# A fused attention and mixture-of-experts kernel: the second layer of its middle part in Strassen form

## The chip, the core and the metric

The kernel runs on one core of a Trainium2 chip. The metric is device time in microseconds (us) of one launch, from the median of several runs. TensorE (PE) multiplies matrices, VectorE (DVE), ScalarE (ACT) and GpSimd (POOL) do elementwise work, SyncE (SP) issues most of the DMA transfers.

## What is computed

Causal attention over 4 batches, 8 heads, 576 positions and head size 64, with a local mask (the last 32 positions) on heads 0 to 3 and a strided one (every 32nd position) on heads 4 to 7. Its output, 2304 tokens of 512 channels, goes through four experts:

```python
p = domain_probs / (domain_probs.sum(-1, keepdims=True) + 1e-09)
out = np.zeros((N, D), dtype=np.float32)
for e in range(E):
    h = np.maximum(x @ w1[e], 0.0)
    out += p[:, e:e + 1] * (h @ w2[e])
```

with N = 2304, D = 512, E = 4 and a hidden size of 1024. All is float32.

## The kernel before, in words

**Precision.** Each float32 operand of a matmul is split into a high part (rounded by ACT to the fp32r type) and a low part (the difference, by DVE or POOL). A product takes three passes: high x high, high x low, low x high. `split` (line 816) makes a pair of instructions: the ACT copy and the difference.

**Units and parts.** An expert's hidden size is halved, so there are 8 units of (512 x 512) weights for each layer. The tokens are in three parts of 384, 896 and 1024 (`TA`, `TBS`, lines 361 and 362).

- First stage: attention for all tokens, mixed with both layers for the first 384 tokens (`plan_first`, line 965), in plain form. The attention output of the other tokens stays in SBUF (`xr`, lines 399 and 403).
- Middle part, 896 tokens (`plan_unit`, line 1293; loop at 1407): the first layer in Strassen form. The weight matrix is cut into quarters a11, a12, a22 and the combinations s1 to s4, the tokens into b11, b21, b22 and t1 to t4 (`plan_x`, line 1040); seven products with 2 halves and 6 matmuls of 448 columns each, instead of eight. The second layer is plain (`plan_mm2`, line 947): 7 tiles of 128 tokens, 12 matmuls of 512 columns for each. `accumulate` (line 932) adds the product times the token's probability into the output tile `acc` straight from PSUM.
- Last part, 1024 tokens (`plan_second`, line 1246): both layers in Strassen form with 512 columns. Here the tokens of the second layer lie along the columns, so the result is transposed (`out_t`) and the probability of a token is a row (`late["p"]`, filled by `plan_p`, line 1236). The two units of one expert are added in `acc`, multiplied by the row, and the sums over experts kept in DRAM (`po`): stored by SP for the first expert, added by an accumulating DMA on POOL's queue for the second, read back and added for the third (lines 1220 to 1230). For the fourth the weights are put on the hidden values instead.

**Weights of the last part.** While the middle part works on a unit, the seven split quarters of its first layer (`plan_keep1`, line 873) and of its second (`plan_keep2`, line 880; three plain ones out of `w2t`, four combinations by way of `wv`) are stored to DRAM (`d1`, `d2`). The last part loads them into the tiles of `wt` and into a ring of four tiles (`plan_ring`, line 1176).

**What sets the order.** Nothing is scheduled on the chip. The class `Plan` (line 44) takes every operation with an engine, a duration, tokens that it reads and writes and a priority (the time at which it is due), and `walk` (line 121) plays a list schedule once, when the program is built: at each step the engine that can start first takes the ready operation with the lowest priority value. The matmuls of the experts keep their written order. An operation of kind "VP" goes to DVE or POOL, one of kind "AD" to ACT or DVE, whichever would end first in that play. DMA transfers have a model of the queue (`transfer`, line 223). The order found this way is fixed on each engine; semaphores do the rest. The last part runs the tasks of `TURN` (line 1090) for each unit: seven products of the first layer ("h"), two of them of the unit after ("next"), then seven of the second ("o").

Of the kernel before, what the change touches and what calls it, by code (L numbers as in the profile page):

```python
# [43 lines left out]
class Plan:  # L44
# [8 lines left out]
    DEEP = 1.26  # L53
    ROW = 1.0
# [6 lines left out]
    def __init__(self, banks, mix):  # L61
        self.ops = []
        self.writer = {}
        self.readers = {}
        self.banks = banks
        self.mix = mix
        self.swing = self.SWING

    def add(self, eng, dur, fn, reads=(), writes=(), prio=0.0, bank=None, moe=False, cols=0, xfer=None, two=False, lead=None, lag=0.0):
# [15 lines left out]
        o.idx = len(self.ops)  # L85
# [35 lines left out]
    def walk(self):  # L121
# [206 lines left out]
def attn_moe_kernel(  # L328
# [59 lines left out]
    d1 = {(u, n): dram.tile([P, 2, 2, 256], F32, name=f"d1{u}{n}") for u in range(2 * E) if u != 2 * E - 2 for n in QUART}  # L388
    d2 = {(u, n): dram.tile([P, 2, 2, 256], F32, name=f"d2{u}{n}") for u in range(2 * E) for n in QUART}
    po = [dram.tile([P, 512], F32, name=f"po{i}") for i in range(TBS[1] // P)]  # L390
    dp = dram.tile([TBS[1] // P * E, P], F32, name="dp")
    prT = const.tile([TBS[1] // P * E, P], F32, name="prT")

    mid_pool = tc.tile_pool(name="mid", bufs=1)
# [3 lines left out]
    raws = {1: mid.tile([P, NKD, FH], F32, name="raw1"), 2: mid.tile([P, NKF, DM], F32, name="raw2")}  # L398
# [417 lines left out]
    def split(src, tok, hi, lo, name, z):  # L816

        need = [tok, "late1"] if name in ("s1", "s2", "s4") or name[:2] == "wv" else [tok]
# [33 lines left out]
    def plan_w1(z, step, plain):  # L852

        def t(i):
            return lambda: tmp["s", i]

        if plain:
            plan_quarter(A11, "raw10", "a11", z)
        total(t(0), A21, A22, ["raw10", "raw11"], "ws0", z + step)
        plan_quarter(t(0), "ws0", "s1", z + step)  # L860
        combine(t(1), t(0), A11, ["raw10", "ws0"], "ws1", z + 2 * step)
        plan_quarter(t(1), "ws1", "s2", z + 2 * step)
        if plain:
            plan_quarter(A12, "raw11", "a12", z + 3 * step)
        combine(t(2), A11, A21, ["raw10"], "ws2", z + 4 * step)
        plan_quarter(t(2), "ws2", "s3", z + 4 * step)
        if plain:
            plan_quarter(A22, "raw11", "a22", z + 5 * step)
        combine(t(0), A12, t(1), ["raw11", "ws1"], "ws0", z + 6 * step)
        plan_quarter(t(0), "ws0", "s4", z + 6 * step)  # L870


    def plan_keep1(u, z):
        for n, nm in enumerate(QUART):
            add("SP", 0.4, lambda nm=nm: nc.sync.dma_start(out=d1[u, nm], in_=wt[nm].bitcast(F32)), [nm + "h", nm + "l"], [f"d1{u}{nm}"],
                z + n, xfer=((1.45, 128),))
# [3 lines left out]
    def plan_keep2(u, z, step):  # L880


        for n, (nm, i, j) in enumerate((("a11", 0, 0), ("a12", 0, 1), ("a22", 1, 1))):
# [3 lines left out]
                [f"w2{2 * j + a}{h}" for a in range(2) for h in "hl"], [f"d2{u}{nm}"], z + 2 + n, xfer=((1.6, 512),))  # L887

        def t(i):
            return lambda: tmp["s", i]  # L890

        def keep(n, nm):
            v = n % 2
            split(t((0, 1, 2, 0)[n]), f"ws{(0, 1, 2, 0)[n]}", lambda: late["wv"][v][:, :, 0], lambda: late["wv"][v][:, :, 1], f"wv{v}", z + n * step)
            add("SP", 0.4, lambda: nc.sync.dma_start(out=d2[u, nm], in_=late["wv"][v].bitcast(F32)), [f"wv{v}h", f"wv{v}l"], [f"d2{u}{nm}"],
                z + n * step + 2, xfer=((1.45, 128),))
# [178 lines left out]
    def pm_of(part):  # L1075
        return 6 * (TBS[part - 1] // 2 + 34) / 2400
# [446 lines left out]
```

## Time and profile before

| | us |
|---|---|
| median of 3 runs (lowest, highest) | 792.45 (792.16, 792.56) |
| the profiled execution | 791.97 |
| its span, first to last instruction | 790.2 |
| first stage, 0 to | 193.6 |
| middle part, 193.6 to | 481.2 |
| last part, 481.2 to | 786 |

The profile is of one execution. Busy time is the time in which an engine works on an instruction. A row of grouped instructions gives source line, engine, operation, "output<-inputs" by the program's names, partitions x elements, count, busy time and mean duration of one in ns. Matmuls are pipelined, so one matmul's duration (0.36 or 0.39 us) overlaps with its neighbours'; what one costs is read from the chain, where consecutive ones are merged.

### The profile page before, as it was taken

To read this page: it belongs to the slowest core of one execution; us is meant where nothing else is said; L and a number is where in the kernel's file an instruction comes from. 1 tells how busy PE (TensorE), PEld (TensorE's weight loads), DVE (VectorE), ACT (ScalarE), POOL (GpSimd) and SP (SyncE) were. 2 spreads that over 40 slices of the span, in tenths; PEclk is the share of its full clock that TensorE was granted. 3 is DMA by queue.
4 is the path that set the end of the run, shared out by engine and by line. 5 is a ranking of instruction groups with operands and counts; after the bars stand their busy time and mean duration, and the time that the engine had idled before them with its cause. 6 is when DMAs were issued, how large, how long until landed. Compare 5 with 4: busy or idle time off the path is not lost.

```text
span 790.2 us, 13778 instructions
## 1 busy us (share of the span) xinstructions
PE 780.6 (99%) x5377; PEld 663.9 (84%) x5377; DVE 585.3 (74%) x807; ACT 361.8 (46%) x662; POOL 340.5 (43%) x261
## 2 busy tenths in 40 slices
PE   8999999999999999999999999999999999999997
PEld 5788888899888889898988888888888888888886
DVE  7888867796888586867768592838774867498885
ACT  4645454653534445263535453735273436442330
POOL 6334223682755162534425170307030753086672
PEclk9999999999999999999999999999999999999999
DMA  9777553157779677775952416737683698559525
GB/s 333 282 269 259 204 176 120 60 201 261 292 276 349 204 293 249 281 265 215 318 219 102 160 40 209 294 116 260 202 327 144 232 172 334 198 189 239 200 81 186
DMA packets 73137, 174.09 MB, mean 220 GB/s; under 512 B 5584, under 2 KB 23664, under 8 KB 73072
## 3 DMA queue, kind: packets, MB, share of 16 engines
q1 hardware_dynamic: 70624, 168.91, 59.5%
q0 software_dynamic: 2304, 4.20, 3.3%
q8 instruction: 42, 0.69, 0.3%
q14 instruction: 23, 0.19, 0.1%
q10 hardware_dynamic: 144, 0.11, 0.0%
HBM read 109.22 MB, written 63.98 MB: 219 GB/s over the span
## 4 chain that ended last, share of the span: by engine, by line
PE 97%; DVE 1%; ACT 0%; issue 0%; POOL 0%; DVEq 0%; ACTq 0%
PE mo L1083 23%; PE mo L930 18%; PE ps L1083 18%; PE sc L1083 15%; PE mo L914 9%; PE ps L930 5%; PE sc L930 5%; PE ps L706 2%; PE ps L674 1%; PE sc L562 1%; PE sc L551 1%; PE mo L1429 0%; PE ps L641 0%; DVE wv L820 0%; DVE mx L579 0%
## 5 line engine op out<-in xcount | busy, mean ns | idle before, releaser
L930 PE MATMUL mo<-w2t,h 128*128 128x512 f32 x336 | 80.8, 389 | 0.0
L930 PEld LDWEIGHTS mo<-w2t,h 128*128 128x128 f32 x336 | 63.1, 188 | 13.0
L930 PE MATMUL mo<-w2t,hs 128*128 128x512 f32 x288 | 70.9, 397 | 0.0
L1152 POOL TENSOR_TENSOR Tt1l<-q,Tt1h 128x512 fp32r<-128x512 f32 x8 | 10.3, 1289 | 134.1 <-ACT Tt1h L1151 134.1
L921 DVE SCALAR_TENSOR_TENSOR h<-c,h 128x448 fp32r<-128x448 f32 x48 | 61.6, 1309 | 2.4 <-ACT h L918 1.0
L930 PEld LDWEIGHTS mo<-w2t,hs 128*128 128x128 f32 x288 | 52.8, 188 | 11.3
L820 POOL TENSOR_TENSOR w2t<-raw,w2t 128x512 fp32r<-128x512 f32 x21 | 31.4, 1505 | 61.2 <-ACT w2t L819 51.1
L1115 DVE TENSOR_TENSOR q<-ps,v 128x512 f32<-128x512 f32 x36 | 24.9, 692 | 39.9 <-PE ps L1083 34.8
L819 ACT ACTIVATE w2t<-raw 128x512 fp32r<-128x512 f32 x60 | 37.4, 631 | 32.7 <-PE mo L930 18.8
L820 POOL TENSOR_TENSOR a<-raw,a 128x512 fp32r<-128x512 f32 x17 | 27.7, 1630 | 57.1 <-DVE c L1318 55.3
L939 DVE SCALAR_TENSOR_TENSOR acc<-mo,pr,acc 128x512 f32<-128x512 f32 x45 | 33.5, 745 | 24.1 <-PE mo L930 23.7
L1117 ACT ACTIVATE q<-q 128x512 f32<-128x512 f32 x36 | 22.8, 632 | 54.3 <-DVE q L1115 53.5
L1156 POOL TENSOR_TENSOR q<-q,q 128x512 f32<-128x512 f32 x26 | 38.2, 1470 | 21.4 <-DVE q L1125 13.6
L914 PE MATMUL mo<-xh,a 128*128 128x384 f32 x192 | 45.6, 340 | 0.0
L819 ACT ACTIVATE wv<-tmp 128x512 fp32r<-128x512 f32 x32 | 20.1, 631 | 53.2 <-POOL tmp L827 8.0
L1156 DVE TENSOR_TENSOR q<-q,q 128x512 f32<-128x512 f32 x38 | 41.3, 1099 | 1.8 <-POOL Tb21l L1152 1.1
L930 PE MATMUL ps<-w2t,h 128*128 128x512 f32 x168 | 40.4, 389 | 0.0
L930 PE MATMUL sc<-w2t,h 128*128 128x512 f32 x168 | 40.4, 389 | 0.0
L1218 DVE TENSOR_TENSOR acc<-sc,acc 128x512 f32<-128x512 f32 x45 | 30.5, 684 | 10.0 <-PE sc L1083 9.9
L1105 ACT ACTIVATE v<-mo 128x512 f32<-128x512 f32 x48 | 28.6, 595 | 18.7 <-PE mo L1083 18.7
L930 PEld LDWEIGHTS ps<-w2t,h 128*128 128x128 f32 x168 | 31.5, 188 | 6.5
L930 PEld LDWEIGHTS sc<-w2t,h 128*128 128x128 f32 x168 | 31.5, 188 | 6.5
(287 smaller groups left out, 2112.4 us busy)
## 6 DMA issues: line engine op xcount, KB each, us to landing
raw<-in_w SPq DMA_DIRECT2D x28, 1024.0 KB, 6.6
qkS<-in_qk_strided SPq DMA_DIRECT2D x16, 329.0 KB, 7.2
out<-acc SPq DMA_DIRECT2D x17, 256.0 KB, 2.0
vstL<-in_v_local SPq DMA_DIRECT2D x6, 640.0 KB, 5.6
vstS<-in_v_strided SPq DMA_DIRECT2D x8, 384.0 KB, 6.1
qkL<-in_qk_local SPq DMA_DIRECT2D x7, 416.0 KB, 6.4
qkL<-in_qk_local SPq DMA_DIRECT2D x10, 208.0 KB, 6.0
raw<-in_w SPq DMA_DIRECT2D x4, 512.0 KB, 7.5
```

The costliest lines, as they stand in the source:

```text
L819: add("ACT", 0.62, lambda: nc.scalar.activation(out=hi(), in_=src(), func=AF.Copy), need, [name + "h"], z)
L820: add("VP", VP, lambda e: engine(e).tensor_tensor(out=lo(), in0=src(), in1=hi().bitcast(F32), op=ALU.subtract), need + [name + "h"], [name ...
L914: nc.tensor.matmul(pt[:, 0:TA], w[:, c % 2, (f % 2) * P:(f % 2) * P + P], (xl if i == 1 else xh)[c], start=j == 0, stop=j == 11)
L921: nc.vector.scalar_tensor_tensor(out=dst(), in0=src(), scalar=0.0, in1=hi().bitcast(F32), op0=ALU.max, op1=ALU.subtract)
L930: nc.tensor.matmul(pt, ht[f][:, ts], wt[f][:, cs], start=j == 0, stop=j == 11)
L939: nc.vector.scalar_tensor_tensor(out=a, in0=pt, scalar=sc, in1=a, op0=ALU.mult, op1=ALU.add)
L1083: nc.tensor.matmul(pt, a[i == 2][:, j, f * P:f * P + P], skewed(b[i == 1][j], TH)[:, cs], start=bool(first) and n == 0, stop=True, skip_gr ...
L1105: add("ACT", TH2 / 1200 + 0.18, lambda: nc.scalar.activation(out=late["u"][i], in_=held[key][:, 0:TH2], func=AF.Copy), [key, "late3"], [f" ...
L1115: add("DVE", DD, lambda: nc.vector.tensor_tensor(out=q(), in0=src(), in1=late["u"][i], op=ALU.add), [key, f"u{i}", "late3"], [tok], min(zz ...
L1117: add("ACT", TH2 / 1200 + 0.2, lambda: nc.scalar.activation(out=q(), in_=q() if nm else src(), func=AF.Relu), ["late3"] + ([] if nm else [ ...
L1156: add("VP", VP, lambda e: engine(e).tensor_tensor(out=dst[0](), in0=a[0](), in1=b[0](), op=ALU.subtract), [a[1], b[1]], [dst[1]], zz - 2.4)
L1218: add("DVE", DD, lambda i=i, key=key: nc.vector.tensor_tensor(out=acc[i], in0=held[key][:, 0:TH2], in1=acc[i], op=ALU.add), [key], tok, zd)
```

## The change

The diff is some 880 lines. What it does:

1. `plan_unit`, `plan_w1`, `plan_keep1`, `plan_keep2`, `open_third` and `plan_second` go. One `plan_part` runs the turns of the old last part for both later parts, with 448 or 512 columns. The second layer of the middle part is thus in Strassen form, its result is transposed, and its probabilities are rows.
2. The plain quarters a11, a12, a22 of both layers are stored to DRAM in the first stage, where they are made (marked `side`, so that the numbering of the other operations stays), and the middle part loads them back.
3. The middle part loads the raw weights again and forms the combinations s1 to s4 (`prep1`, `prep2`, one temporary tile for each layer, used in place), uses them and stores them for the last part.
4. In both later parts the sums over experts are formed in DRAM. In the middle part none of the experts has its weights on the hidden values, so there are three accumulating transfers for each of 8 output tiles.
5. The operands `T` of the second layer share five tiles that are given out in turn, the ring has five tiles. The product a22 of the first layer is no longer copied to SBUF first: ACT and DVE read it from PSUM three times (`put_raw`, `sub_raw`), save in the last two units of the last part.
6. The tokens of the last part are stored to DRAM (`dx`) late in the first stage and loaded into the raw weight tiles when the middle part no longer needs them (`plan_x2`).
7. In the planner a transfer is issued at most 5 us ahead of the modelled queue after 200 us (`DEEPER`). The scratch memory of POOL's DMA descriptors is 1024 instead of 4096 bytes.

```diff
-            if o.xfer is not None and o.start is None and wire < 200:
-                t = max(t, wire - self.DEEP)
+            if o.xfer is not None and o.start is None:
+                t = max(t, wire - (self.DEEP if wire < 200 else self.DEEPER))
...
+    def prep1(u, nm, z):
+        chain_z[0] = z - 1.5
+        chain(lambda: tmp["s", 0], (A11, A12, A21, A22), "raw1", "ws0", nm)
+        plan_quarter(lambda: tmp["s", 0], "ws0", nm, z)
+        if u != LAST1:
+            keep1(u, nm, z + 6)
...
+    def prep2(u, nm, i, z):
+        chain_z[0] = z - 1.5
+        chain(lambda: tmp["s", 1], (B11, B12, B21, B22), "raw2", "ws1", nm)
+        split(lambda: tmp["s", 1], "ws1", lambda: late["ring"][i][:, :, 0], lambda: late["ring"][i][:, :, 1], f"ring{i}", z)
+        add("SP", 0.4, lambda: nc.sync.dma_start(out=d2[u, nm], in_=late["ring"][i].bitcast(F32)), [f"ring{i}h", f"ring{i}l"], [f"d2{u}{nm}"],
+            z + 6, xfer=((1.45, 128),))
...
+        def put_raw():
...
+                    add("ACT", TH / 1200 + 0.17, lambda j=j, hi=hi: nc.scalar.activation(out=hi(), in_=raw(j)(), func=AF.Relu),
+                        [key, "late2"], [f"T{i}h{j}"], zz - RAWT)
+                    add("DVE", vp[0], lambda j=j, hi=hi, lo=lo: nc.vector.scalar_tensor_tensor(
+                        out=lo(), in0=raw(j)(), scalar=0.0, in1=hi().bitcast(F32), op0=ALU.max, op1=ALU.subtract),
+                        [key, f"T{i}h{j}"], [f"T{i}l{j}"], zz - RAWT)
...
+            if not weighted:
+                add("VP", vp, lambda e, av=av, c=c: engine(e).tensor_tensor(
+                    out=av(), in0=av(), in1=late["p"][group % 2][:, c * TH:c * TH + TH], op=ALU.mult), [f"pb{group % 2}"], tok, zd + 10)
+                d, dt = po[part, i], f"po{part}{i}"
                 if group == 0:
+                    add("SP", 0.4, lambda av=av, d=d: nc.sync.dma_start(out=d, in_=av()), tok, [dt], zd + 18, xfer=((0.8, 128),))
+                elif group < (NG - 1 if part == 1 else NG - 2):
+                    add("POOL", 1.27, lambda av=av, d=d: nc.gpsimd.dma_start(out=d, in_=av(), accum_op=ALU.add), tok, [dt], zd + 18,
+                        xfer=((1.3, 128),))
                 else:
+                    add("POOL", 1.27, lambda av=av, d=d: nc.gpsimd.dma_start(out=av(), in_=d, accum_op=ALU.add), [dt], tok, zd + 18,
+                        xfer=((1.3, 128),))
...
         plan_w1_plain(z - 2)
+        for n, nm in enumerate(("a11", "a12", "a22")):
+            keep1(u, nm, z + 4 + n, True)
         plan_load(2, u, z - 10)
         plan_w2(z + 8)
+        keep2(u, z + 14)
         plan_first(u, z)
...
+    first_order = [NU - 1, NU - 2] + list(range(NU - 2))
+    second_order = [LAST1, LAST1 - 1] + list(range(LAST1 - 1)) + [NU - 2, NU - 1]
+    z = plan_part(1, first_order, z)
+    for c in (0, 2, 1, 3):
+        k = 1 + c % 2
+        add("SP", 0.4, lambda c=c, k=k: nc.sync.dma_start(
+            out=raws[k].rearrange("p k f -> p (k f)")[:, c // 2 * 1024:c // 2 * 1024 + 1024], in_=dx[c]), [f"dx{c}"], [f"raw{k}{c // 2}"],
+            z - 20, xfer=((1.5, 128),))
+    plan_x2(z)
+    plan_part(2, second_order, z)
```

The loads of raw weights in the middle part stand in `plan_part` and `plan_ring`: those of the first layer behind the sum for s3 of the unit before, due 14 us and 4 us ahead of the first product that needs them; those of the second layer likewise behind its s3.

## Rows read from the trace of the kernel before

**Rows 1.** The page's first part: busy us, share, instructions of each engine.

```profile
PE 780.6 (99%) x5377; PEld 663.9 (84%) x5377; DVE 585.3 (74%) x807; ACT 361.8 (46%) x662; POOL 340.5 (43%) x261
```

**Rows 2.** Busy time by stretches: start:end, length, engines, granted clock, DMA share, GB/s.

```profile
20.00:100.00 80.00, 78.48 (x1381) 67.00 (x1381) 67.12 (x125) 40.96 (x82) 25.38 (x21) 1.00 0.71 255
100.00:160.00 60.00, 60.00 (x836) 51.27 (x825) 43.12 (x70) 33.98 (x70) 26.41 (x21) 1.00 0.35 122
0.00:193.60 193.60, 188.47 (x2684) 159.37 (x2685) 149.41 (x258) 97.75 (x195) 84.51 (x82) 1.00 0.62 220
193.60:481.20 287.60, 287.24 (x1345) 252.01 (x1344) 216.93 (x271) 130.84 (x235) 128.11 (x87) 1.00 0.64 228
481.20:786.00 304.80, 304.80 (x1351) 252.51 (x1349) 218.17 (x276) 133.25 (x232) 127.91 (x92) 1.00 0.64 215
```

**Rows 3.** Waits of PE: the middle part's only one, and one of the first stage.

```profile
PE mo L1083 <- ACT u L1305: 0.4, 1, 0.4
PE ps L726 <- DMA vstL<-in_v_first: 0.9, 1, 0.9
```

**Rows 4.** The chain: start, us, what; middle part (first and second layer), last part.

```profile
268.51 1.20 PE mo L1083 x6
285.65 2.72 PE ps L930 x12
508.57 2.72 PE mo L1083 x12
```

**Rows 5.** Middle part, groups by line and shape on DVE and ACT.

```profile
L921 DVE SCALAR_TENSOR_TENSOR h<-c,h 128x448 fp32r<-128x448 f32 x48 | 61.6, 1309 | 2.4 <-ACT h L918 1.0
L820 DVE TENSOR_TENSOR wv<-tmp,wv 128x512 fp32r<-128x512 f32 x24 | 26.7, 1113 | 2.7 <-ACT wv L819 2.5
L820 DVE TENSOR_TENSOR s<-tmp,s 128x512 fp32r<-128x512 f32 x12 | 8.2, 685 | 4.4 <-ACT s L819 4.4
L1318 DVE TENSOR_TENSOR c<-mo,u 128x448 f32<-128x448 f32 x24 | 14.7, 613 | 9.2 <-PE mo L1083 9.2
L921 DVE SCALAR_TENSOR_TENSOR h<-mo,h 128x448 fp32r<-128x448 f32 x8 | 4.9, 608 | 0.0
L1305 ACT ACTIVATE u<-mo 128x448 f32<-128x448 f32 x24 | 13.1, 544 | 22.7 <-PE mo L1083 22.7
```

**Rows 6.** Busy time in four stretches with DVE and POOL both pressed; columns as in rows 2.

```profile
204.00:215.00 11.00, 10.64 (x51) 9.21 (x50) 11.00 (x13) 6.72 (x13) 10.69 (x8) 1.00 0.64 254
312.00:324.00 12.00, 12.00 (x58) 10.65 (x58) 11.60 (x15) 7.09 (x14) 10.21 (x7) 1.00 0.90 332
614.70:639.20 24.50, 24.50 (x110) 20.28 (x109) 22.41 (x28) 8.53 (x15) 19.16 (x15) 1.00 0.67 188
160.00:181.00 21.00, 21.00 (x110) 19.45 (x109) 19.54 (x22) 11.06 (x21) 18.80 (x13) 1.00 0.57 199
```

**Rows 7.** Last part, in order of time: start, us, engine, line, tile, count.

```profile
577.94 3.45 POOL L1152 TENSOR_TENSOR Tb22l<-q,Tb22h 128x512 fp32r<-128x512 f32 x2
580.16 3.48 DVE L1152 TENSOR_TENSOR Tt2l<-q,Tt2h 128x512 fp32r<-128x512 f32 x2
612.38 1.29 POOL L1152 TENSOR_TENSOR Tt1l<-q,Tt1h 128x512 fp32r<-128x512 f32 x1 [29.29 <-ACT Tt1h L1151]
621.64 0.68 DVE L1218 TENSOR_TENSOR acc<-sc,acc 128x512 f32<-128x512 f32 x1
631.70 1.01 POOL L1226 DMA_DIRECT2D po<-acc  x1 [2.79 <-DVE acc L1221]
```

**Rows 8.** DMA queues (packets, MB, share of 16 engines), landing times (us), the fullest stretch.

```profile
q1 hardware_dynamic: 70624, 168.91, 59.5%
q0 software_dynamic: 2304, 4.20, 3.3%
raw<-in_w SPq DMA_DIRECT2D x28, 1024.0 KB, 6.6
10.00:20.00 10.00, 8.72 (x158) 6.54 (x162) 9.61 (x26) 7.23 (x17) 8.28 (x13) 1.00 1.03 388
```

More of the change, by code (lines that the diff above doesn't have):

```diff
@@ L53 @@
     DEEP = 1.26
+    DEEPER = 5.0
     ROW = 1.0
@@ L84, in add @@
         o.nxt = []
-        o.idx = len(self.ops)
+        o.idx = self.number
+        if side:
+            o.idx = 100000 + len(self.ops)
+        else:
+            self.number += 1
         o.prio += SHIFT.get(o.idx, 0.0)
@@ L873, in plan_keep1, with chain @@
[L873 to L876, printed above, removed]
-    B11, B12, B21, B22 = ((lambda i=i, j=j: raw_quarter(i, j, 2)) for i in range(2) for j in range(2))
-    def plan_keep2(u, z, step):
+    LAST1 = NU - 3
+    def chain(t, src, tok, ws, nm):
+        x11, x12, x21, x22 = src
+        z = chain_z[0]
+        if nm == "s1":
+            total(t, x21, x22, [tok + "0", tok + "1"], ws, z)
+        elif nm == "s2":
+            combine(t, t, x11, [tok + "0", ws], ws, z)
+        elif nm == "s4":
+            combine(t, x12, t, [tok + "1", ws], ws, z)
+        else:
+            combine(t, x11, x21, [tok + "0"], ws, z)
@@ L1189, in plan_o, with settle @@
+    def settle():
+        while todo_T and (free_T or not todo_T[0][0]):
+            todo_T.pop(0)[1]()
+    def plan_o(part, u, step, slot, group, last, z, due):
+        TH, dz = TBS[part - 1] // 2, pm_of(part)
+        DD = TH / 960 + 0.15
+        vp = (TH / 960 + 0.157, TH / 400)
+        t0 = sum(TBS[:part - 1])
         a, b, kk, first_in = STEPS[step]
         r, c = {"P1": (0, 0), "P2": (0, 0), "s1": (1, 1), "s3": (1, 1), "s2": (0, 1), "s4": (0, 1), "a22": (1, 0)}[step]
+        T = slot_T.pop(b)
+        rhs = lambda: [[late["T"][T][:, h, j] for j in range(2)] for h in range(2)]
+        lhs = lambda: [late["ring"][slot][:, :, h] for h in range(2)]
+        weighted = part == 2 and group == NG - 1
@@ L1215, in plan_o @@
-            if n == 1 and group < NG - 1:
-                add("AD", ad(TH2), lambda e, i=i, key=key: copy(e, lambda: acc[i], key, lambda pt: pt[:, 0:TH2]), [key], tok, zd)
-            else:
-                add("DVE", DD, lambda i=i, key=key: nc.vector.tensor_tensor(
-                    out=acc[i], in0=held[key][:, 0:TH2], in1=acc[i], op=ALU.add), [key], tok, zd)
-            if n == (2 if (r, c) == (1, 0) else 4) and group < NG - 1:
-                add("VP", VP, lambda e, i=i, c=c: engine(e).tensor_tensor(
-                    out=acc[i], in0=acc[i], in1=late["p"][group % 2][:, c * TH2:c * TH2 + TH2], op=ALU.mult), [f"pb{group % 2}"], tok, zd + 1.5)
+            add("PE", dz, lambda f=f, key=key: product(lhs(), rhs(), f, key, first_in, TH),
+                need, [key], zz, key if first_in else None, True, 6 * TH)
@@ new lines, in plan_o @@
+            tok = [f"acc{i}0"]
+            av = lambda i=i: acc[i][:, 0:TH]
+            n = acc_count[part, group, i] = acc_count.get((part, group, i), 0) + 1
+            if n == 1 and not weighted:
+                add("AD", ad(TH), lambda e, av=av, key=key: copy(e, av, key, lambda pt: pt[:, 0:TH]), [key], tok, zd)
+            else:
+                add("DVE", DD, lambda av=av, key=key: nc.vector.tensor_tensor(
+                    out=av(), in0=held[key][:, 0:TH], in1=av(), op=ALU.add), [key], tok, zd)
@@ L1355, in masks @@
+        return zz
     def masks():
```

482 lines of the change are left out of this document (226 added, 256 removed).

## The prediction

> **What bounds the kernel now.** I read the share of busy time first [rows 1]: TensorE (PE) is busy 99% of the span, VectorE (DVE) 74%, GpSimd (POOL) 43%. A whole-span share hides stages, so next came the table by stretches [rows 2]. The stages are: attention beside the first 384 tokens (0 to 193.6 us), the middle part of 896 tokens (193.6 to 481.2), the last part of 1024 tokens (481.2 to 786). PE is busy 287.24 of 287.60 us in the middle part and 304.80 of 304.80 in the last, at granted clock 1.00, the upper of its two levels (2.4 GHz). Its waits in the middle part are a single one of 0.4 us [rows 3]. So the time of the middle part is its matmuls and nothing else, and the chain of work gives their price [rows 4]: six matmuls of 448 columns take 1.20 us (0.200 each), twelve of 512 columns take 2.72 us (0.227 each).
>
> **The change part by part.**
>
> *Matmuls removed.* In the middle part the second layer of one unit is now 7 token tiles x 12 matmuls = 84 matmuls of 512 columns. In Strassen form it is 7 products x 2 halves x 6 = 84 matmuls of 448 columns. Over 8 units 672 matmuls each become 0.227 - 0.200 = 0.0267 us shorter: **-17.9 us**. A unit then needs 168 x 0.200 = 33.6 us of PE, against 287.6 / 8 = 35.95 us now. Nothing takes matmuls from the other stages: the last part's 1344 matmuls x 0.227 are already its whole 304.8 us, so no gain is possible there.
>
> *Vector work in the middle part.* This is what could become the new bound, so I count instructions per unit from the code. Removed: 6 adds, 8 relu-minus instructions and 7 accumulations on DVE, and 23 instructions that go to DVE or POOL (4 + 4 sums and differences, 7 + 8 splits): 44. Added in their place: on DVE alone, all reading PSUM, 6 adds of parked products, 4 for the last product of the first layer (taken straight from PSUM), 10 adds into the output tiles: 20 of 448 columns. On DVE or POOL: 6 differences, 12 splits, 4 products with the probabilities (448 columns), and 16 sums, differences and splits of weights (512 columns): 38. Together 58 instead of 44, in a unit that PE wants to finish in 33.6 instead of 35.95 us. ScalarE gets 26 instructions of 448 and 8 of 512 columns, at most 22 us of 33.6, with 0.54 us for the shorter [rows 5] and 0.1 more for the longer: no bound.
>
> How fast do DVE and POOL together work when both are pressed? Four stretches of the trace show it [rows 6], DVE and POOL each over three quarters busy: 21 instructions in 11.0 us, 22 in 12.0, 35 in 21.0, and in the last part 43 in 24.5, of which 5 are DMA issues, so 38. That is 0.52, 0.55, 0.60 and 0.645 us for one. For 58 the first three give 30.4, 31.6 and 34.8 us. The fourth is all 512 columns; with 0.613 / 0.69 for the 42 shorter ones [rows 5, 7] it gives 16 x 0.645 + 42 x 0.573 = 34.4. So the bounds are 30.4 and 34.8 us against PE's 33.6. The two upper rows are nearest: the fourth runs the very instructions that come into the middle part, the third is the longest row with weight splits. I take 34.6, one us more than PE needs: **+8.0 us** over 8 units. The ends are 0 (PE hides it all) and, from the port below, some 28.
>
> *The port that DVE and POOL share.* Two rows show what pressing both costs [rows 7]: two splits on DVE took 3.48 us while two on POOL took 3.45, 1.74 us each, where a DVE split alone takes 0.69 [rows 5] and a POOL one 1.29. In the middle part now, `h<-c,h` takes 1309 ns where the same instruction from PSUM takes 608, and `wv` 1113 where the splits of `s` take 685 [rows 5]: 48 x 0.70 + 24 x 0.43 = 44 us of DVE, by 87 POOL instructions [rows 2], 0.51 us for each. With 18 of the 38 shared instructions on POOL (a third of all work, as in the second stretch), 18 such pairs and 2 more on DVE take 32.6 us, which 33.6 just holds.
>
> The Trainium skill, page "SBUF — State Buffer", section "SBUF: two separate sides", has a rule against this change: the port pair of the two engines is "an exclusive lock", held by whoever starts first for a whole instruction, also against DVE instructions with two operands in SBUF. By that rule and the durations alone (1.29 and some 0.65 us) the 18 and 20 instructions would hold the port for 36.2 us, and the sum would be 784.0 - 8.0 + 8 x 2.6 = 797. The trace agrees that each side is held up, but its pairs take 1.74 us and not 1.94. It is the second rival below, worked out there from rows.
>
> *POOL's queue.* 24 accumulating DMA issues are new in the middle part, 3 for each output tile, at 1.0 us of POOL each [rows 7], 3 us per unit. Behind them on POOL stand splits that PE waits for. I put their cost inside the 34.6: POOL was idle over half of the middle part. The wait that comes with them (each for its product with the probabilities) is set some 8 us after that product in the order, so nothing should queue for long.
>
> *Transfers.* The hardware queue moved 168.91 MB in 59.5% of the span, 2.78 us per MB, so 512 KB take 1.46 us; an accumulating transfer of 256 KB takes 3.3% / 16 of the span, 1.63 us [rows 8]. The first stage gets 42 stores of plain quarters (six for each of seven units; the eighth's are there today) and 4 of the last part's tokens: 46 x 1.46 = 67 us, on top of 0.62 x 193.6 = 120: 187 of 193.6 us, 97%. From 20 to 100 us the queues are busy 0.71 x 80 = 57 us [rows 2] and some 3.5 units add 31: 8 us more than fit, to be caught up after 100 us, where the share is 0.35. The stores stand on SP ahead of the next weight and attention loads. Two things hide them: the attention loads run ahead of use, and a unit's weight buffers are rewritten only a unit (some 20 us) later. The ends are 0 and 8 us; I take **+1.0**, nearest to the 0.9 us that PE once waited for a load there [rows 3]. A gain is excluded: the matmuls of the stage stay. In the middle part 42 stores go (61 us), 45 reloads come (66), and accumulations (24 x 1.63 x 0.875 = 34), plain partial sums, probabilities and tokens (16): 0.64 x 287.6 = 184 becomes 239 of 269 us, 89%. Reloads are issued 14 us ahead, and 1 MB of weights takes 6.6 to land [rows 8]: hidden, unless the next raw weights come late, since their one buffer is held until the last sum of the unit before is formed.
>
> *Turn to the last part.* Its operands are formed from tokens that come back from DRAM (4 x 1.46 us) in 22 vector instructions, while PE does the seven output products of the last unit (7 x 2.4 = 16.8 us). The reload and the instructions at 0.6 us are 19 us, so the ends are 0 and 2.2 us; I take **+0.5**, nearest to today's turn, which shows no wait. In the last part four instructions per unit become DVE's alone; DVE is busy 218 of 304.8 us there, so nothing.
>
> *Sum.* The profiled execution: 791.97 us with a span of 790.2 and 1.8 around it. 791.97 - 17.9 + 8.0 + 1.0 + 0.5 = 783.6. The median of the runs stands 0.5 above the profiled one: **784.0 us**. A difference of 0.2% (1.6 us) is about what a measurement of this kernel can tell from none.
>
> **The rivals.**
>
> *PE stays the bound.* If the 58 instructions run at the rate of the first two stretches (30.4 to 31.6 us), or the planner finds order enough, PE never waits: 792.45 - 17.9 = 774.5, to 777 with small waits at the turns. For it: PE lost 0.4 us in all in those four stretches [rows 3, 6]. Against it: they lasted 10 to 25 us, not 270.
>
> *The shared port makes it slower.* POOL takes about a third of the work when pressed (7 of 22 [rows 6]), 18 of 58. The 40 left on DVE at 0.59 us (30 at 0.573, 10 at 0.645, as above) are 23.6 us. Each POOL instruction then adds what it holds DVE up: at today's 0.51 us the unit is 32.8 us, at the full 1.05 us (1.74 - 0.69) it is 42.5. It decides at 0.67 us: there the unit is 35.7 us and the gain is gone with the 1.5 us above. At 0.75 it is 37.1, 8 x 3.5 = 28 us over PE's need: 792.45 - 17.9 + 28 = 802.5. For it: DVE has fewer gaps than today, so a held port finds it waiting more often. Against it: 20 of DVE's instructions read PSUM, and such a one kept its 0.68 us while POOL worked [rows 7]. The Trainium skill's rule above belongs to this rival; its 797 lies on the way to the 802.5.
>
> *Transfers set the pace.* At 97% and 89% each late load of raw weights costs PE directly. If the 8 us of the first 100 us are all paid, with the vector term, it is 774.5 + 8 + 8 + 0.5 = 791: no change. For it: the two shares. Against it: a 10 us stretch moved 388 GB/s [rows 8], the middle part would need about 290 (65.6 MB now and 12.8 more in 269 us).
>
> **How the numbers follow.** Forecast (PE waits about a us per unit; 777 to 790.8): 0.45. PE stays the bound: 0.22. Port, slower: 0.24. Transfers: 0.09, of which 0.07 no change and 0.02 slower. So faster 0.67, same 0.07, slower 0.26. The range reaches from PE's floor, 774.0, to 800.0, which leaves out the dearer part of the port's rival, about 1 in 8. The forecast's own range is 777 to 790.8.
>
> **What would show it right or wrong.** Right: in the middle part matmuls of 448 columns only, a unit of 34 to 35 us, PE waiting on splits (the low parts of the `T` and weight tiles), DVE over 90% busy, 58 instructions per unit. PE waits of next to nothing there and 774 to 777: the vector term was wrong. Middle part over 287 us with `T` or difference instructions at 1.1 us and more on DVE: the port. PE waits on DMA before 193 us or on raw weights: transfers. The prediction falls altogether if the last part grows from 304.8 us.

## The result and the profile after

The changed kernel takes 803.35 us, median of 4 runs (801.88 to 806.41), against 792.5 for the kernel before in the same session: a ratio of 1.0141, 95% interval 1.0108 to 1.0174. It is slower by 1.4%; the prediction was 784.0, with 800.0 as the upper end of its range. The profiled execution took 802.37 us.

First the page's busy times, then the stages in the table by stretches (columns as in [rows 2]).

```profile
PE 774.2 (97%) x5374; PEld 668.0 (83%) x5377; DVE 629.1 (79%) x870; ACT 380.7 (48%) x719; POOL 442.0 (55%) x351
```

```profile
0.00:198.70 198.70, 190.55 (x2680) 158.91 (x2684) 151.88 (x262) 95.79 (x191) 86.57 (x83) 1.00 0.91 327
198.70:487.20 288.50, 276.78 (x1345) 255.48 (x1345) 248.21 (x318) 158.61 (x306) 225.01 (x170) 0.98 0.80 273
198.00:340.00 142.00, 141.78 (x708) 132.04 (x707) 124.18 (x157) 80.34 (x154) 114.21 (x82) 1.00 0.86 316
360.00:400.00 40.00, 37.78 (x179) 34.31 (x178) 35.19 (x46) 23.64 (x46) 27.17 (x21) 0.96 0.93 333
400.00:440.00 40.00, 35.28 (x168) 31.89 (x167) 32.39 (x41) 18.36 (x36) 29.27 (x26) 0.95 0.83 240
440.00:480.00 40.00, 35.43 (x163) 32.32 (x162) 34.85 (x48) 22.77 (x44) 33.33 (x25) 0.93 0.46 153
```

Three things are to be seen. PE has fallen from 99% [rows 1] to 97%. For the first 142 us of the middle part, more than four units, PE is busy 141.78 of 142 us although DVE and POOL run 157 and 82 instructions in them, some 57 for each 33.6 us: nothing but PE sets the pace there. After some 340 us PE loses 2 to 5 us in every 40 and its granted clock falls under 1. The waits of PE in the middle part, and the one of the last part (waited for: us, times, longest):

```profile
PE sc L1097 <- ACT acc L469: 5.7, 2, 4.6
PE sc L1097 <- DVE acc L1294: 3.3, 1, 3.3
PE ps L1097 <- DVE q L1145: 1.3, 1, 1.3
PE sc L1097 <- DVE T L1184: 1.1, 1, 1.1
PE ps L1097 <- DMA ring<-d27a: 0.2, 1, 0.2
...
PE sc L1097 <- ACT acc L469: 2.6, 1, 2.6
```

What changes at 340 us is that POOL begins to issue accumulating transfers. One burst of them in POOL's order of time, and what then happens up to PE's longest wait (start, us, engine, line, tile, count, [idle before it <- what ended that]; "issue" is time for which the profile shows no reason):

```profile
415.56 1.78 POOL L1305 DMA_DIRECT2D po<-acc  x2
418.42 1.09 POOL L1305 DMA_DIRECT2D po<-acc  x1
423.84 0.86 POOL L1305 DMA_DIRECT2D po<-acc  x1 [4.33 <-issue]
427.38 0.86 POOL L1305 DMA_DIRECT2D po<-acc  x1 [2.69 <-issue]
427.95 1.61 POOL L832 TENSOR_TENSOR tmp<-raw,tmp 128x512 f32<-128x512 f32 x1
429.21 1.46 POOL L1184 TENSOR_TENSOR T<-q,T 128x448 fp32r<-128x448 f32 x1
430.71 4.42 DVE L1226 TENSOR_TENSOR q<-q,q 128x448 f32<-128x448 f32 x2 [6.52 <-POOL T L1184]
434.62 1.04 ACT L1182 ACTIVATE T<-q 128x448 fp32r<-128x448 f32 x2 [8.65 <-DVE q L1226]
437.02 0.95 ACT L469 ACTIVATE acc<-sc 128x448 f32<-128x448 f32 x2
437.60 4.85 PE L1097 MATMUL sc<-T,ring 128*128 128x448 f32 x12 [4.59 <-ACT acc L469]
...
444.79 2.56 PE L1097 MATMUL sc<-T,ring 128*128 128x448 f32 x12
```

Three issues go out in 4 us, then POOL stands still for 4.33 us in front of the fourth and 2.69 us in front of the fifth. Behind them stood a difference of weights and a split of `T`; DVE waited 6.52 us for that split, ACT 8.65 us for DVE, and the copy that frees PSUM for PE came behind ACT's splits. PE lost 4.59 us by the wait and some more after it: the next twelve matmuls take 4.85 us where a later twelve take 2.56. The granted clock was 0.57 from 435 to 440 us, close to the lower of its two levels (1.2 GHz).

Where the time went, by stage, from the profiled executions (the last column is an experiment below, the fastest of its runs):

| us | before | after | after with 2048 bytes |
|---|---|---|---|
| first stage | 193.6 | 198.7 | 197.8 |
| middle part | 287.6 | 288.5 | 275.2 |
| from there to the end of the launch | 310.8 | 315.2 | 312.7 |
| sum | 792.0 | 802.4 | 785.7 |

So 5.1 us came in the first stage, 4.4 in the last part, and the middle part gained nothing, where 8 x 33.6 = 268.8 us of matmuls left room for 18.8. The 4.4 us of the last part are nearly all the one wait of 2.6 us and the twelve matmuls behind it, which take 4.54 us where others there take 2.88. (The expectations below count the middle part to 488.4 us and so give it 289.7.)

### The profile page after: what moved, and what is told of

Same layout as the page of the kernel before. It is cut to its first block, busy times and chain, and to the rows that moved or that the text cites. A ratio compares the mean times of both kernels' runs of the same rounds, so it can differ in the third digit from the quotient of the medians.

```text
span 800.6 us, 14154 instructions
## 1 busy us (share of the span) xinstructions
PE 774.2 (97%) x5374; PEld 668.0 (83%) x5377; DVE 629.1 (79%) x870; ACT 380.7 (48%) x719; POOL 442.0 (55%) x351
## 4 chain that ended last, share of the span: by engine, by line
PE 76%; POOL 7%; DVE 7%; issue 5%; DMA 3%; ACT 1%; SPq 1%; DVEq 0%; POOLq 0%; ACTq 0%
PE ps L1097 21%; PE mo L1097 21%; PE sc L1097 17%; PE mo L927 7%; PE mo L911 6%; PE ps L714 2%; DVE T L1184 1%; DVE q L1226 1%; POOL T L1184 1%; DMA ring<-d27a 1%; POOL tmp L832 1%; DMA vstL<-in_v_first 1%; DVE tmp L832 1%; DMA raw<-dx 1%; POOL acc L1308 1%
## 5 line engine op out<-in xcount | busy, mean ns | idle before, releaser
L1184 POOL TENSOR_TENSOR T<-q,T 128x448 fp32r<-128x448 f32 (+1 forms) x87 | 123.5, 1433 | 135.8 <-ACT T L1182 135.8
L1097 PE MATMUL sc<-T,ring 128*128 128x448 f32 (+2 forms) x774 | 182.1, 385 | 12.6 <-ACT acc L469 8.2
L1097 PEld LDWEIGHTS sc<-T,ring 128*128 128x128 f32 x774 | 148.6, 194 | 36.0 <-ACT acc L469 9.4
L1182 ACT ACTIVATE T<-q 128x512 fp32r<-128x512 f32 (+1 forms) x196 | 113.6, 601 | 109.2 <-POOL q L1226 40.0
L1184 DVE TENSOR_TENSOR T<-q,T 128x512 fp32r<-128x512 f32 (+1 forms) x109 | 117.2, 1089 | 22.3 <-ACT T L1182 21.5
L1145 DVE TENSOR_TENSOR q<-ps,v 128x448 f32<-128x448 f32 (+1 forms) x96 | 62.3, 654 | 40.5 <-PE ps L1097 35.6
L1097 PE MATMUL mo<-T,ring 128*128 128x512 f32 (+1 forms) x396 | 90.7, 377 | 0.1
L1097 PEld LDWEIGHTS mo<-T,ring 128*128 128x128 f32 x396 | 75.0, 190 | 11.1 <-POOL T L1184 0.5
L1226 DVE TENSOR_TENSOR q<-q,q 128x448 f32<-128x448 f32 (+1 forms) x58 | 71.3, 1243 | 13.4 <-POOL T L1184 12.7
L1226 POOL TENSOR_TENSOR q<-q,q 128x512 f32<-128x512 f32 (+1 forms) x42 | 61.7, 1474 | 21.9 <-DVE q L1151 13.2
L1294 DVE TENSOR_TENSOR acc<-sc,acc 128x512 f32<-128x512 f32 (+1 forms) x85 | 54.2, 651 | 11.8 <-PE sc L1097 11.6
```

What stands on the lines that cost most here:

```text
L1097: nc.tensor.matmul(pt, a[i == 2][:, j, f * P:f * P + P], skewed(b[i == 1][j], TH)[:, cs], start=bool(first) and n == 0, stop=True, skip_gr ...
L1145: add("DVE", DD, lambda: nc.vector.tensor_tensor(out=q(), in0=src(), in1=late["u"][i][:, 0:TH], op=ALU.add), [key, f"u{i}", "late2"], [tok ...
L1182: add("ACT", TH / 1200 + 0.17, lambda src=src, hi=hi: nc.scalar.activation(out=hi(), in_=src(), func=AF.Copy), [tok, "late2"], [f"T{i}h{j} ...
L1184: add("VP", vp, lambda e, src=src, hi=hi, lo=lo: engine(e).tensor_tensor(out=lo(), in0=src(), in1=hi().bitcast(F32), op=ALU.subtract), [to ...
L1226: add("VP", vp, lambda e, d=d, x=x, y=y: engine(e).tensor_tensor(out=d[0](), in0=x[0](), in1=y[0](), op=ALU.subtract), [x[1], y[1]], [d[1] ...
L1294: add("DVE", DD, lambda av=av, key=key: nc.vector.tensor_tensor(out=av(), in0=held[key][:, 0:TH], in1=av(), op=ALU.add), [key], tok, zd)
```

## The experiments

The theory after this reading: POOL's gaps "<- issue" are the shrunken scratch memory of its DMA descriptors (1024 instead of 4096 bytes, point 7 of the change), and the first stage is longer by its 42 stores. The rivals: the accumulating transfers as such, the port of DVE and POOL, or the order.

**Scratch memory 2048.** The order of every engine is that of the changed kernel.

```diff
-    nc = bacc.Bacc("TRN2", target_bir_lowering=False, num_devices=1, dynamic_dma_scratch_size=1024)
+    nc = bacc.Bacc("TRN2", target_bir_lowering=False, num_devices=1, dynamic_dma_scratch_size=2048)
```

> The changed kernel with 2048 instead of 1024 bytes of descriptor scratch; the order of every engine is the same. Ring theory (POOL's queue stands still while about three accumulating transfers are under way, and what POOL owes PE comes late): the gaps of 1.1 to 4.6 us in front of the accumulating issues shrink below 0.5 us, PE's waits in the middle part fall from 11.4 us to under 2, the middle part from 289.7 to 269 to 273 us, the turn at 517 us costs nothing, in all 780 to 785 us. Port theory (DVE and POOL block each other, which makes both late): the same instructions meet in the same order, so 800 to 805 us as before. Transfers theory: 800 to 805 us.

Measured: 789.05 us (785.72 to 790.66, 7 runs), ratio to before 0.9952 (0.9935 to 0.9968). One number takes 14.3 us off the changed kernel and makes it faster than the kernel before. POOL at the same burst, then the table by stretches and PE's waits in the middle part:

```profile
409.57 1.76 POOL L1305 DMA_DIRECT2D po<-acc  x2
410.79 1.87 POOL L832 TENSOR_TENSOR tmp<-raw,tmp 128x512 f32<-128x512 f32 x1
412.41 2.85 POOL L1305 DMA_DIRECT2D po<-acc  x3
```

```profile
197.80:473.00 275.20, 270.62 (x1346) 251.29 (x1345) 247.36 (x318) 158.43 (x306) 228.01 (x169) 1.00 0.83 286
198.00:340.00 142.00, 142.00 (x711) 132.91 (x710) 124.75 (x158) 81.33 (x156) 114.75 (x83) 1.00 0.87 315
400.00:440.00 40.00, 39.82 (x197) 36.32 (x196) 39.87 (x48) 22.73 (x45) 38.55 (x29) 1.00 0.83 246
```

```profile
PE sc L1097 <- DVE acc L1294: 3.3, 1, 3.3
PE ps L1097 <- DVE q L1145: 1.1, 1, 1.1
PE ps L1097 <- DVE acc L1294: 0.2, 1, 0.2
...
PE sc L1097 <- ACT acc L469: 1.7, 1, 1.7
```

Five issues go out with no gap, and the 4.6 us wait is gone. The time stayed above the 780 to 785 expected: the first stage and the last unit of the middle part still cost more than they should, with 4.6 us of waits in the middle part where under 2 were expected. They are taken up below. Nor did the turn cost nothing: 1.7 us of wait are left in the last part. The chain of work behind this one holds no stall of POOL: an output tile is read back from DRAM for 12.3 us and stored for 10.9 us before ACT may write it again. The seven runs differ by 5 us, and their mean granted clocks lie between 1.000 (785.72 us) and 0.994.

**Scratch memory 1536**, the same line.

> Only the scratch memory of POOL's DMA descriptors is changed, to 1536 bytes. Theory (a number of transfers under way that grows with the scratch memory): with 1024 bytes POOL stood still from the fourth or fifth issue of a burst on, 22 us in all (14.0 on the issues from acc to po, 6.8 to 12.6 in the two parts), with 2048 not at all; with 1536 the stall comes later in a burst and is a third or less, 0 to 7 us, and the time is 788 to 794 us. Rival (some fixed threshold between 1024 and 2048, or a stall that has nothing to do with the size): either all of the 1024 stall, 800 to 806 us, or none, 786 to 790.

Measured: 786.12 us in its one run. The groups of POOL's issues in the changed kernel (busy us, mean ns | idle before, what ended it), then the burst of eight at the turn with 1024, 1536 and 2048 bytes:

```profile
L1305 POOL DMA_DIRECT2D po<-acc x24 | 22.1, 973 | 21.8 <-issue 14.0 <-DVE acc L1299 6.0 <-DVE acc L1294 1.0
L1308 POOL DMA_DIRECT2D acc<-po x16 | 14.4, 983 | 17.4 <-issue 6.8 <-DVE acc L1299 5.7 <-DVE q L1145 2.1
```

```profile
491.62 2.73 POOL L1308 DMA_DIRECT2D acc<-po  x3
498.95 0.87 POOL L1308 DMA_DIRECT2D acc<-po  x1 [4.60 <-issue]
```

```profile
478.25 4.50 POOL L1308 DMA_DIRECT2D acc<-po  x5
484.43 0.86 POOL L1308 DMA_DIRECT2D acc<-po  x1 [1.68 <-DVE q L1145]
488.91 0.89 POOL L1308 DMA_DIRECT2D acc<-po  x1 [3.62 <-issue]
```

```profile
478.62 6.32 POOL L1308 DMA_DIRECT2D acc<-po  x7
488.56 0.88 POOL L1308 DMA_DIRECT2D acc<-po  x1 [3.62 <-PE mo L1097]
```

The profile puts 20.8 us down to "issue" with 1024 bytes, 3.6 with 1536 and none with 2048. These labels are inferred, and the landings of the transfers say more. Three, five and seven issues go out in a row, and the next one starts 0.31, 0.26 and 0.26 us after the first of them has landed (at 498.64, 484.17 and 488.30 us), whatever the label says; so the 3.62 us put down to PE are the same stall with 2048 bytes. In none of the traces here are more than three accumulating transfers (224 or 256 KB each) under way with 1024 bytes, five with 1536 or seven with 2048; the kernel before, with 4096, never has more than four, and no issue waits for a landing there. The scratch memory holds a number of transfers that grows with its size, as expected. The time lies under the theory's 788 to 794 us; from a single run, it can't be told from that with 2048.

**The kernel before with 1024 bytes**, to see whether the size alone costs anything there.

```diff
-    nc = bacc.Bacc("TRN2", target_bir_lowering=False, num_devices=1, dynamic_dma_scratch_size=4096)
+    nc = bacc.Bacc("TRN2", target_bir_lowering=False, num_devices=1, dynamic_dma_scratch_size=1024)
```

> The kernel before with 1024 instead of 4096 bytes of descriptor scratch, same order. Ring theory: its two bursts of eight accumulating transfers (631 and 707 us) get gaps of 1 to 4 us in front of the fourth and later ones; the time stays within 2 us, since POOL was idle for long stretches around them. Port theory: no gaps, 792 us.

Measured: 792.94 us, ratio 1.0001 (0.9992 to 1.0011). The same stretch of POOL's order as in the last of [rows 7]:

```profile
637.44 0.89 POOL L1226 DMA_DIRECT2D po<-acc  x1 [0.95 <-DVE acc L1218]
640.28 0.88 POOL L1226 DMA_DIRECT2D po<-acc  x1 [1.96 <-DVE acc L1218]
```

These are the fourth and fifth issue of the burst, and they come later here too: the gaps of 0.95 and 1.96 us are put down to an accumulation, but each issue starts 0.25 us after a landing (637.18 and 640.03 us), and with 4096 bytes both gaps were 0.46. But nothing that PE needs soon stands behind them. The size is harmless until a full queue has work behind it.

**No accumulating transfers in the middle part.** Its partial sums go out as plain stores by SP; the sums over experts are left out.

```diff
-                if group == 0:
+                if group == 0 or part == 1:
```

> Leaves out the sums over experts in the middle part: its 24 accumulating transfers on POOL's queue become plain stores on SP's queue. Ring theory: as with the larger ring, middle part 269 to 273 us, 780 to 785 us in all. If the time that POOL spends on issuing (24 x 0.9 us) is the cost and not the ring, this run gains the same but the larger ring does not. Port theory: within 5 us of the changed kernel.

Measured: 791.76 us (790.03 to 797.06, 10 runs), ratio 0.9994 (0.9977 to 1.0011): 11.6 us under the changed kernel, with the scratch memory still at 1024 bytes. POOL's idle time under "issue" in front of its accumulating transfers is down to 2.7 us. It fell short of the 780 to 785 expected. Its order is that of the changed kernel up to some 340 us and another one behind, and in the profiled run, its slowest, the first stage ended only at 202.2 us, with a granted clock of 0.96 from 20 to 100 us; so the rest isn't told apart here. That the transfers as such are not the cost is shown by the larger scratch memory: with 2048 bytes all of them are there, and the time is lower.

**The first stage without its stores.** The 42 stores of plain quarters are left out and the loads read the last unit's quarters, with 1024 and with 2048 bytes.

```diff
-            keep1(u, nm, z + 4 + n, True)
+            if u == NU - 1:
+                keep1(u, nm, z + 4 + n, True)
...
-        keep2(u, z + 14)
+        if u == NU - 1:
+            keep2(u, z + 14)
```

> Leaves out the 42 stores of plain quarters in the first stage; the reloads stay and read the eighth unit's quarters instead. Transfers theory: the first stage falls from 198.7 back to 193.6 to 194.5 us, and nothing else changes: 797 to 799 us. If the stores also made the middle part late, its 289.7 us fall too. Ring theory: the middle part keeps its waits behind the accumulating transfers, 286 to 291 us.

> c_nostore (the 42 stores of plain quarters in the first stage left out, the planner told so, the later loads read the last unit's quarters, so the output is another) with scratch 2048 instead of 1024; the order of every engine is that of c_nostore. Theory (the stores cost the first stage some 4 us in whichever form, as order or as waits on DMA, and c_nostore lost its gain in POOL's queue of DMA issues): no gap at the accumulating issues, first stage to 194 to 194.6 us, the middle part some 273 to 279 us with the turn's waits, time 781 to 786 us. Rival (the order that the planner makes without the stores is bad in the middle part for other reasons, as in g_free_stores, where a ring tile's load and splits of T came late): 788 to 797 us.

Measured: 807.37 us (ratio 1.0192) with 1024 bytes and 794.28 (1.0014, 1.0005 to 1.0023) with 2048. Neither total is what the theory gave (the second lies in its rival's range): the planner makes another order for the whole program, in which a tile of the ring and splits of `T` come late in the middle part. Waits with 2048 bytes:

```profile
PE sc L1097 <- DVE T L1185: 4.3, 4, 1.8
PE ps L1097 <- DVE q L1146: 3.4, 3, 2.1
PE ps L1097 <- DMA ring<-d27a: 3.1, 1, 3.1
```

Two things hold all the same. The pair is a second measurement of the scratch memory under an order of its own: 13.1 us. And the first stage ended at 194.3 us in the first of the two profiles, 196.8 in the second, though its order is the same: it varies from run to run. The granted clock from 20 to 100 us was 1.00 in the first and 0.98 in the second, which goes some way to explain it.

**The stores' bytes alone.** The stores stay in place but carry 32 KB each; no engine's order changes (2048 bytes). The diff shows the stores of the first layer; those of the second are shortened likewise.

```diff
-nc.sync.dma_start(out=d1[u, nm], in_=wt[nm].bitcast(F32))
+nc.sync.dma_start(out=d1[u, nm][:, 0, 0, 0:64], in_=wt[nm][:, 0, 0, 0:64].bitcast(F32)) if side and u != NU - 1 else nc.sync.dma_start(out=d1[u, nm], in_=wt[nm].bitcast(F32))
```

> Scratch 2048 as in a_ring2048, and the 42 stores of plain quarters in the first stage stay where they are on SP but carry 32 KB each instead of 512 KB (the later loads read the last unit's quarters, so the output is another). Every engine has the order of a_ring2048. Theory (the first stage is longer because the stores' bytes fill the DMA queues from 20 to 140 us): the first stage ends at 193.5 to 194.5 us instead of 197.8, the rest stays, and the time is 784 to 786 us. Rival (it is longer because of SP's order or of the changed order of the attention's matmuls, not of bytes): the first stage still ends at 197 to 198 us and the time stays at 788 to 790.

Measured: 787.44 us, ratio 0.9934 (0.9918 to 0.9951), which overlaps that with whole stores. The queues are relieved (a share of 0.97 from 20 to 100 us before the edit), yet the first stage ends at 197.5 us. One row of its table by stretches, and three of PE's order of time:

```profile
20.00:100.00 80.00, 78.25 (x1259) 65.77 (x1262) 60.63 (x110) 39.77 (x80) 28.95 (x27) 1.00 0.68 229
```

```profile
156.70 0.92 PE L714 MATMUL ps<-pTS,vstS 54*64 54x54 f32 x48
188.01 1.55 PE L927 MATMUL mo<-w2t,hs 128*128 128x512 f32 x6
189.80 7.84 PE L927 MATMUL mo<-w2t,hs 128*128 128x512 f32 x30 [0.24 <-ACT hs L915]
```

In the kernel before, these two places read:

```profile
141.59 0.92 PE L706 MATMUL ps<-pTS,vstS 54*64 54x54 f32 x48
185.37 8.36 PE L930 MATMUL mo<-w2t,hs 128*128 128x512 f32 x36
```

The rival was right on the first stage: with the bytes gone its end stays, so it is the order. (The time lies between the two expectations.) The attention's last matmuls stand 15 us later, and the last 36 matmuls of the stage take 9.46 us to the next product (188.01 to 197.47) instead of 8.20, behind a late relu: the chain leads from them to its difference on DVE, which stands behind a split of the middle part's weights. That is 1.3 of the 3.9 us; where the others arise isn't shown.

**The order without the cost of the stores.** The planner is told that they take no time; the bytes are all there (2048 bytes of scratch memory). The diff shows one of three such lines.

```diff
-            z, xfer=((1.45, 128),), side=side)
+            z, xfer=((0.01 if side else 1.45, 128),), side=side)
```

> Scratch 2048. The planner is told that the first stage's stores (plain quarters and the last part's tokens) take no time on the DMA queue; the stores themselves stay whole. So the order of the first stage is the one without their cost, and the bytes are all there. Theory (e_small_stores took the bytes away and the first stage still ended at 197.5 us, so it is the order that the planner made in view of the stores, with the attention's matmuls some 15 us later and the middle part's first operands crowding the last products, that costs the 4 us): the first stage ends at 194 to 195.5 us, and the time is 784 to 788 us, unless the new order of the middle part brings waits of its own. Rival (bytes): the first stage still ends at 197.5 us or later with PE waits on DMA, time 789 us or more.

Measured: 796.57 us, ratio 1.0045 (1.0027 to 1.0063). Now PE waits for transfers in the first stage, which ends at 199.8 us with the queues full (share 1.00 from 20 to 100 us, granted clock 0.98):

```profile
PE sc L570 <- DMA qkL<-in_qk_local: 3.6, 2, 3.0
```

The rival's signs came true here, as the other side's did with the small stores; neither is the whole of it. The bytes do cost: as waits if the order ignores them, as a worse order if it makes room for them. Either way the stage ended some 4 to 6 us later than in the kernel before, one profile each. In the middle part this order has the late ring tile and splits of the kernels without stores.

**The last unit of the middle part.** The 22 instructions that form the last part's tokens work on 128 columns instead of 512; no engine's order changes (2048 bytes).

```diff
+        cut = lambda f: (lambda: f().rearrange("p (a b) -> p a b", b=64)[:, 0:8:7])
...
-                    out=lo(), in0=src(), in1=hi().bitcast(F32), op=ALU.subtract), [need, f"{nm}h{j}"], [f"{nm}l{j}"], zz)
+                    out=cut(lo)(), in0=cut(src)(), in1=cut(hi)().bitcast(F32), op=ALU.subtract), [need, f"{nm}h{j}"], [f"{nm}l{j}"], zz)
```

> Scratch 2048, every engine in the order of a_ring2048, but the 22 sums, differences and low parts that form the last part's tokens at the turn work on 128 columns instead of 512 (the other columns keep old values, so the output is another). Theory (DVE and POOL are full from 400 to 475 us because these 22 come on top of the 58 of a unit): the wait of 3.3 us on DVE's accumulation near 461 us falls under 1 us, the waits between 435 us and 480 us from some 4.6 us to under 1.5, and the middle part from 275 to 279 us down to 269 to 271; time 780 to 783 us. Rival (the unit's own 58 instructions, or pairs of DVE and POOL instructions that hold each other up, are enough): waits of over 2.5 us stay and the time is 785 us or more.

Measured: 783.16 us, ratio 0.9878 (0.9866 to 0.9891), 5.9 us under the median with whole instructions. PE's only wait there:

```profile
PE sc L1097 <- DVE acc L1294: 2.3, 1, 2.3
```

The time is just above the theory's 780 to 783 us, but the wait near 461 us shrank only from 3.3 to 2.3 us and the middle part of the profiled run is 274.9 us, not 269 to 271. Part of the wait is thus the unit's own. The twelve matmuls behind it took 4.09 us here and 2.65 in the kernel with whole instructions, which hides some of the gain; from the middle part's end to the end of the launch the profiled run took 310.6 us instead of 312.7, without the wait of 1.7 us. The rows of the 2048-byte kernel show how DVE and POOL meet there:

```profile
453.72 3.04 POOL L1184 TENSOR_TENSOR T<-q,T 128x448 fp32r<-128x448 f32 x2
454.17 3.08 DVE L1226 TENSOR_TENSOR q<-q,q 128x448 f32<-128x448 f32 x2
...
460.88 2.65 PE L1097 MATMUL sc<-T,ring 128*128 128x448 f32 x12 [3.28 <-DVE acc L1294]
```

Two differences on DVE take 3.08 us beside two splits on POOL, 1.54 each, where the shortest such difference takes 0.61: the pairs of [rows 7], in the 4 us ahead of a PE wait.

**Another order at the turn** (2048 bytes): the same 22 instructions due 5 us later and 7 us earlier.

```diff
-    XLEAD = 5.0
+    XLEAD = 0.0
```

> Scratch 2048, and the instructions that form the last part's tokens at the turn get a priority 5 us later (lead 0 instead of 5). Only the order of DVE, ACT and POOL between about 435 and 480 us differs from a_ring2048. Theory (at the turn DVE and POOL have more work than PE leaves time for, so an order only moves the wait): the 3.3 us wait on DVE's accumulation near 461 us shrinks to 0 to 2 us and a wait on the last part's operands of 1 to 4 us comes after 473 us; time 787 to 791. Rival (the order alone makes the wait): the waits at the turn fall from 6.1 us in all to under 2 and the time is 784 to 786.

> Scratch 2048, and the same instructions get a priority 7 us earlier (lead 12 instead of 5). Theory (too much work for DVE and POOL at the turn): the waits of PE between 435 and 480 us stay at 5 to 8 us in all and those behind it fall from 1.7 us to under 1; time 788 to 791. Rival (order alone): waits from 435 us to the end under 3 us, time 784 to 787.

Measured: 790.32 us (789.01 to 790.86) and 788.40 (786.75 to 790.02): no gain over 789.05. With 0 the 3.3 us wait stays, and behind the turn came only 0.6 us on a weight tile, so that part of the expectation missed. With 12 it is 1.7 us, and one on `q` grows to 2.1: 3.8 us, where the theory gave 5 to 8 and its rival under 3. (A wait of 1.4 us on a ring tile stands at 235 us, where the order is unchanged.) The lead of 12 on top of the order of the kernel whose planner was told that stores take no time:

> g_free_stores with the priority of the turn's instructions 7 us earlier (lead 12 as in x_12). If the turn's waits can be had out by order as x_12 hinted (3.8 us of waits there instead of 4.6 and 1.7): 1 to 2 us under g_free_stores. If DVE and POOL are simply full at the turn: the same as g_free_stores within 1 us.

Measured: 797.97 us, against 796.57: no help there either. No kernel here that computes the whole function is clearly faster than the changed kernel with 2048 bytes: with a lead of 12 the interval (0.9916 to 0.9954) overlaps its own (0.9935 to 0.9968), and 1536 had a single run.

## Why the prediction was wrong

*POOL's queue* is the step that failed. The prediction put the 24 new issues inside the vector work at 1.0 us each and said that "nothing should queue for long". It looked for a wait on the product with the probabilities; the wait was on the issue itself. The list of the change named the scratch memory of 1024 bytes, and the sum gave it no term. These hold three transfers at a time. With them POOL stood 20.8 us or more in front of issues, the middle part of the profiled execution took 13.3 us longer than with 2048 bytes (288.5 against 275.2), and the median of the whole rose by 14.3. The Trainium skill, page "DMA: Bandwidth & Descriptors", section "SWDGE vs HWDGE vs iDMA", says that GpSimd appends descriptors to rings in SBUF which the DMA engines drain; a full ring fits what the runs show, but that page gives no size and no wait. It adds that DVE, in a mode with two ports, locks GpSimd out of that state. That isn't the cause here: with 2048 bytes DVE did the same work and the burst at 410 us has no gap, and a delayed issue starts 0.25 to 0.35 us after a landing.

*Matmuls removed*: right. A run of twelve starts 2.40 us after the one before (444.79 to 447.19 in the changed kernel), which is 0.200 us for each, as summed.

*Vector work*, +8.0: too dear. In the first 142 us of the middle part PE waits 0.22 us with 1024 bytes and never with 2048, with DVE busy 87 to 88% and POOL 80 to 81% of the time. The rival "PE stays the bound" was right for more than four units of eight.

*The shared port*: its rival gave 802.5 us, next to what was measured, by another mechanism. The same instructions in the same order give 789 with the larger scratch memory. The sign that the prediction set for it came true all the same (a middle part over 287 us, `T` and difference instructions on DVE at 1190 and 1227 ns), so the sign was a bad one: with 2048 bytes these take 1130 and 1267 ns and the middle part 275.2 us. The Trainium skill's rule of an exclusive lock, page "SBUF — State Buffer", section "SBUF: two separate sides", gave 36.2 us per unit; the trace doesn't agree over those first units, which keep PE's 33.6. There the margin is small: by an estimate from the shortest durations (1.14 and 0.61 us for 448 columns, 1.29 and 0.69 for 512) the rule would hold the port for some 145 us in those 142. Pairs that hold each other up are there, but they cost time only where POOL or DVE is already late: after a stall, and in the last unit.

*Transfers*, +1.0: mis-sized. The first stage grew by 5.1 us in the changed kernel and by 3.6 to 4.2 in four others with its order (to 197.2 to 197.8 us); two more ended at 199.9, and one at 202.2. The bounds of 0 and 8 us held the changed kernel and all of these but the last (8.6), and the value was taken too near to the lower one. Nor was the cost where it was looked for: hardly a wait on DMA, but a different order of attention and relu.

*Turn*, +0.5: mis-sized. With 2048 bytes the middle part is 275.2 - 268.8 = 6.4 us over its matmuls, 4.6 us of it waits in its last 40 us. The sum counted the 22 instructions against PE's seven products as if DVE and POOL were free; from 400 to 440 us DVE is busy 39.87 of 40.

*Last part*, 0: mis-sized, and its growth was the sign by which the prediction was to fall altogether. Its matmuls are the same, but it grew by 4.4 us with 1024 bytes and by 1.9 with 2048, of which waits of PE are 2.6 and 1.7.

With these in place (-17.9, vector work 0, first stage +4.2, turn +6.4, last part 312.7 - 310.8 = +1.9) the sum is 791.97 - 5.4 = 786.6 for 2048 bytes; its profiled execution took 785.7. This is no test, since all but the first term are read from that kernel, but it shows that no large cost is left out. The forecast of the middle part, -17.9 + 8.0 + 0.5 = -9.4, lies near that kernel's -12.4 by luck: 8.0 us too much for the vector work and 5.9 too little for the turn.

What stays open: how far the first stage's end moves by chance. Kernels with one order ended it from 194.3 to 196.8, and from 197.2 to 202.2 us. The two ends of 196.8 and 202.2 go with a granted clock of 0.98 and 0.96 from 20 to 100 us; at 1.00 throughout kernels of the second order still lie between 197.2 and 199.9. So the split of its 4 us between order and bytes is rough. Why the planner's order without the stores is late in the middle part wasn't pursued.

## What to carry to other kernels

A small setting in a diff (a buffer, a queue's depth) needs a term in the sum like any instruction: ask how many of its users are under way at once, and what stands behind the one that doesn't fit. An engine that both computes and issues transfers turns a full queue into a stall of its next instruction; look for idle time that the profile puts down to "issue" or to nothing, and follow who waited behind it. A stage that gets transfers can be lengthened without a single wait on DMA where a planner rearranges the work around them.

## What was not expected of the hardware

With 1024 bytes of scratch memory POOL issued three accumulating transfers of 224 KB and then stood up to 4.6 us in front of the next, until the first had landed; with 1536 bytes it was five, with 2048 seven. The profile can put such a stall down to an engine that has nothing to do with it. A PE wait of 3 to 5 us costs more than itself: after 4.59 us the next twelve matmuls took 4.85 us instead of 2.56, and the granted clock of the two stretches that this touches was 0.95 and 0.93. After the same 3.28 us wait at the turn the twelve took 3.98 us in the changed kernel, 2.65 in the kernel with 2048 bytes and 4.82 in that with small stores, so this second cost comes and goes:

```profile
473.81 3.98 PE L1097 MATMUL sc<-T,ring 128*128 128x448 f32 x12 [3.28 <-DVE acc L1294]
```
